# Loading the first four chunks of a gated recurrence in 112-row transfers, the first gate tensor in two column halves

## Chip, cores and metric

The kernel runs on one core of a Trainium2 chip. The metric is the device time of one execution, in microseconds. The core has five engines that work side by side: TensorE (PE; its weight loads are listed as PEld), VectorE (DVE), ScalarE (ACT), GpSimd (POOL) and SyncE (SP), which here issues all transfers between device memory and the on-chip memory. Sixteen DMA engines carry the transfers. On-chip tiles have up to 128 partitions (rows).

## What is computed

A gated linear recurrence for 4 batches and 8 heads, 768 steps of 48 channels, and then a multiplicative feed-forward block (FFN) on 3072 tokens of width 384:

```python
f = 1.0 / (1.0 + np.exp(-f_logit))
state = zeros((B, H, D, D))
for t in range(S):
    state = f[:, :, t, :, None] * state + np.einsum('bhd,bhe->bhde', k[:, :, t], v[:, :, t])
    y[:, :, t] = np.einsum('bhd,bhde->bhe', q[:, :, t], state)
x = y.transpose(0, 2, 1, 3).reshape(B * S, H * D)
a = x @ w1
b = x @ w2
out = ((a * b) @ w3) @ w_out
```

The kernel cuts each sequence into chunks of 128 steps, 24 chunks in all (6 for each batch). In a chunk it multiplies q by the running product of the gates from the chunk's start (a forward scan), and k by the running product toward the chunk's end (a backward scan), so that the products within a chunk become matmuls under a causal mask, and only one state passes from chunk to chunk. w3 and w_out are folded into one matrix on the chip.

## The kernel before

The inputs q, k and f_logit lie in device memory as `[chunk, 2, 48, 512]`: the heads in two groups (even and odd, `par`), 48 channels each, and for every channel 4 heads x 128 steps. On the chip a chunk's tile has R = 112 rows: group 0 in rows 0 to 47, group 1 in rows 64 to 111. Rows 48 to 63 belong to neither group; their results are not used, but what stands in them goes through the scans and products, so they are filled with values that do no harm (0 for q and k, 30 for f). The first four chunks have tiles of their own, so that all their loads can be issued at the start.

A small planner (`plan.add(engine, cost, emit, deps, prio)`) lays all work out in time by the estimated costs and emits it engine by engine in that order; the costs in the code are its estimates. The two functions that matter here are `setup`, with the fills, and `front`, with the loads, the sigmoid, the scans and the two products. The loads of one core's SyncE are tied to eight completion semaphores in turn: the ninth load waits until the first has landed.

```python
def rows(par):
    return slice(64 * par, 64 * par + D)
# ...
    floor = keep.tile([R, NQ], F32, name="floor")
    back = keep.tile([R, NQ], F32, name="back")
    gate = [keep.tile([R, NQ + 1], F32, name=f"gate{i}") for i in range(2)]
    qs, ks, fs = ([keep.tile([R, NQ], F32, name=f"{nm}{i}") for i in range(n)] for nm, n in (("q", 3), ("k", 2), ("f", 2)))
    # ...
    def idle(n):

        to = ps_f.tile([P, TB], F32, name=f"f{NF - 1}")[:, 0:TH]
        for _ in range(n):
            nc.tensor.matmul(to, lhsT=floor[:, 0:P], rhs=floor[:, 0:TH], start=True, stop=True)

    plan.add("PE", 7.8, lambda: idle(9), prio=-1e8)

    def setup():
        nc.scalar.activation(warm, nc.const_aps.tensor(0.0, (R, 1), F32), AF.Sigmoid)
        for i in range(2):
            if i == 0:
                nc.gpsimd.memset(ks[i][32:64], 0.0)
                nc.gpsimd.memset(qs[i][32:64], 0.0)
                make_identity(nc, ident)
            else:
                nc.gpsimd.memset(fs[i][32:64], 30.0)
        nc.gpsimd.memset(early[32:64, 2:4], 30.0)
        nc.gpsimd.memset(early[32:64, 0:2], 0.0)
        nc.gpsimd.memset(qs[2][32:64], 0.0)
        nc.gpsimd.memset(qs[3][32:64], 0.0)
        nc.vector.memset(floor, FLOOR)
        nc.vector.memset(heads(floor)[:, :, 0], 1.0)
        nc.vector.memset(back, 0.0)
        for t in gate:
            nc.vector.memset(t[:, NQ : NQ + 1], 0.0)
        nc.vector.memset(ks[1][32:64], 0.0)
        nc.vector.memset(qs[1][32:64], 0.0)
        for t in sb:
            nc.vector.memset(t, 0.0)

        nc.gpsimd.memset(perm, 0.0)
        # ... ten copies of parts of ident into perm, on GpSimd
    def moves(n, size, rate, emit, deps, prio, late=0.0):


        for j in range(n):
            i = plan.add("SP", 0.45, (lambda: None) if j else emit, [d] if j else deps, prio - j * 1e-3, takes=["lane"], lag=0.6)
            d = i
            t = plan.add("DMA", size / n / rate, lambda: None, [i], prio - j * 1e-3, lag=1.3 + late, frees=[i])
        return t

    def front(u):

        s, t = st[u], tk[u]
        n0 = need(u)

        def load(dst, src):
            def emit():
                if dst is fs[0] and u == 0:

                    nc.sync.dma_start(dst[0:64], src[u].rearrange("two d n -> (two d) n")[0:64])
                    nc.sync.dma_start(dst[rows(1)], src[u, 1])
                    return
                for par in range(2):
                    nc.sync.dma_start(dst[rows(par)], src[u, par])
            return emit

        fu, qu, ku = (x[u if u < 4 else u % n] for x, n in ((fs, 2), (qs, 3), (ks, 2)))

        def free(n, *names):

            if u < 4:
                return []
            return asked[8:9] + [tk[u - n if u - n >= 4 else u % n][nm] for nm in names]

        t["lf"] = moves(2, 197, 250, load(fu, f_logit), free(2, "g"), n0 - 30)
        t["lk"] = moves(2, 197, 250, load(ku, k), free(2, "k"), n0 - 29.5)
        t["lq"] = moves(2, 197, 250, load(qu, q), free(3, "q"), n0 - 29)

        def load_v():
            s["v"] = at(12288 + NQ, DM) if u == 3 else loads.tile([P, DM], F32, name="vt")
            loaded(s["v"], u)

        t["lv"] = moves(
            1 if u < NPE else 3, 197, 320, load_v, [] if u == 3 else past(u, 4 if u in (4, 5, 6) else 3, "v", "s"),
            n0 - (28.2, 28.2, 28.2, 29.6, 12)[min(u, NPE)],
        )

        def gates():
            nc.scalar.activation(gate[u % 2][:, 0:NQ], fu, AF.Sigmoid)

        t["g"] = plan.add("ACT", 0.65, gates, [t["lf"]] + past(u, 2, "r") + past(u, 3, "G"), n0)
        if u % NCH and "G" in tk[u - 1]:
            tk[u - 1]["G"]["deps"].append(t["g"])

        def forward():
            s["P"] = one.tile([R, NQ], F32, name="fwd")
            nc.vector.tensor_tensor_scan(s["P"], gate[u % 2][:, 0:NQ], floor, 0.0, ALU.mult, ALU.max)

        t["p"] = plan.add("DVE", 1.25, forward, [t["g"]] + past(u, 1, "q", "i", "l"), n0)

        def last():
            nc.scalar.copy(lasts[:, u], heads(s["P"])[:, :, C - 1])

        t["l"] = plan.add("ACT", 0.2, last, [t["p"]], n0)

        def ends():
            nc.vector.reciprocal(heads(back)[:, :, C - 1], heads(s["P"])[:, :, C - 1])

        t["i"] = plan.add("DVE", 0.18, ends, [t["p"]] + past(u, 1, "r"), n0)

        def scale_q():
            s["Q"] = work3.tile([R, NQ], F32, name="Q")
            nc.vector.tensor_tensor(s["Q"], qu, s["P"], ALU.mult)

        t["q"] = plan.add("DVE", 0.7, scale_q, [t["p"], t["lq"]] + past(u, 3, "v", "a"), n0 + 0.1)

        def backward():
            s["R"] = one.tile([R, NQ], F32, name="bwd")
            nc.vector.tensor_tensor_scan(
                s["R"][:, ::-1], gate[u % 2][:, NQ:0:-1], back[:, ::-1], 0.0, ALU.mult, ALU.max
            )

        t["r"] = plan.add("DVE", 1.25, backward, [t["i"]] + past(u, 1, "k"), n0)

        # ... K = k * R (VectorE), then pairs(u): K^T Q on PE into pa; A = copy of pa (ScalarE);
        # causal select on A (GpSimd); values, from_state, update (PE); S, G, sb: the running state;
        # moved (PE, with perm) and settled (ScalarE): xt, the input of the FFN
# ...
    setup()
    for u in range(NU):
        if u <= NPE:
            front(u)
        if u >= NPE:
            if not (u > NPE and together(u - 1)):
                begin(u)
            if u + 1 < NU:
                front(u + 1)
        rest(u)
        if u == NPE - 1:
            weights()
        if u == NU - 1:
            looked = plan.add("DVE", 1.0, judge, [tk[i]["y"] for i in range(NU)], -20)
            sent = moves(1, 0.4, 250, told, [looked], 0, 20.0)
            judged = plan.add("DVE", 0.2, decided, [moves(1, 0.4, 250, heard, [sent], 0, 20.0)], -20)
        if u % UB == UB - 1:
            ffn(u // UB)
    ready_at = 0.0
    for t in plan.order():
        if t["eng"] == "PE" and t["at"] < FULL:
            n = int((t["at"] - ready_at) / 0.43)
            if ready_at and n:
                idle(n)
            ready_at = t["end"]
        plan.got = t.get("got")
        t["emit"]()
    return blk[NB - 1]["outside"]
```

D = 48, R = 112, C = 128, NQ = 512, HP = 4, NPE = 4, NU = 24, FLOOR = 2^-60. `idle` gives PE matmuls whose result is never read, to keep it at work before the first real ones.

Of the kernel before, what the change touches and what calls it, by code (L numbers as in the profile page):

```python
# [36 lines left out]
F32 = mybir.dt.float32  # L37
# [3 lines left out]
ALU = mybir.AluOpType  # L41
AF = mybir.ActivationFunctionType
# [3 lines left out]
P = 128  # L46
# [4 lines left out]
R = 64 + D  # L51
# [138 lines left out]
def rows(par):  # L190
    return slice(64 * par, 64 * par + D)
# [15 lines left out]
def ranged(ctx, tc, q, k, f_logit, v, w1, w2, w3, w_out, out, ident, w12, wc, left):  # L207
# [65 lines left out]
    def idle(n):  # L273

        to = ps_f.tile([P, TB], F32, name=f"f{NF - 1}")[:, 0:TH]
        for _ in range(n):
            nc.tensor.matmul(to, lhsT=floor[:, 0:P], rhs=floor[:, 0:TH], start=True, stop=True)

    plan.add("PE", 7.8, lambda: idle(9), prio=-1e8)

    def heads(t):
        return t.rearrange("p (h c) -> p h c", c=C)

    def setup():
        nc.scalar.activation(warm, nc.const_aps.tensor(0.0, (R, 1), F32), AF.Sigmoid)
        for i in range(2):
            if i == 0:
                nc.gpsimd.memset(ks[i][32:64], 0.0)
                nc.gpsimd.memset(qs[i][32:64], 0.0)
                make_identity(nc, ident)  # L290
            else:
                nc.gpsimd.memset(fs[i][32:64], 30.0)
        nc.gpsimd.memset(early[32:64, 2:4], 30.0)
        nc.gpsimd.memset(early[32:64, 0:2], 0.0)
        nc.gpsimd.memset(qs[2][32:64], 0.0)
        nc.gpsimd.memset(qs[3][32:64], 0.0)
        nc.vector.memset(floor, FLOOR)
        nc.vector.memset(heads(floor)[:, :, 0], 1.0)
        nc.vector.memset(back, 0.0)
        for t in gate:  # L300
            nc.vector.memset(t[:, NQ : NQ + 1], 0.0)
        nc.vector.memset(ks[1][32:64], 0.0)
        nc.vector.memset(qs[1][32:64], 0.0)
        for t in sb:
            nc.vector.memset(t, 0.0)

        nc.gpsimd.memset(perm, 0.0)
        for i, (kc, hp) in enumerate(met):
            for par in range(2):
                for r, t, at_, n in runs(2 * hp + par):  # L310
                    if t == kc:
                        a = 64 * par + at_
                        nc.gpsimd.tensor_copy(perm[:, i, r : r + n], ident[0:R, a : a + n])
# [22 lines left out]
# [8 lines that stand above are left out]
# [11 lines left out]
    def front(u):  # L355

        s, t = st[u], tk[u]
        n0 = need(u)

        def load(dst, src):  # L360
            def emit():
                if dst is fs[0] and u == 0:

                    nc.sync.dma_start(dst[0:64], src[u].rearrange("two d n -> (two d) n")[0:64])
                    nc.sync.dma_start(dst[rows(1)], src[u, 1])
                    return
                for par in range(2):
                    nc.sync.dma_start(dst[rows(par)], src[u, par])  # L368
# [7 lines that stand above are left out]
                return []  # L376
            return asked[8:9] + [tk[u - n if u - n >= 4 else u % n][nm] for nm in names]

        t["lf"] = moves(2, 197, 250, load(fu, f_logit), free(2, "g"), n0 - 30)
        t["lk"] = moves(2, 197, 250, load(ku, k), free(2, "k"), n0 - 29.5)  # L380
        t["lq"] = moves(2, 197, 250, load(qu, q), free(3, "q"), n0 - 29)

        def load_v():
            s["v"] = at(12288 + NQ, DM) if u == 3 else loads.tile([P, DM], F32, name="vt")
# [4 lines that stand above are left out]
            n0 - (28.2, 28.2, 28.2, 29.6, 12)[min(u, NPE)],  # L389
        )  # L390

        def gates():
            nc.scalar.activation(gate[u % 2][:, 0:NQ], fu, AF.Sigmoid)  # L393

        t["g"] = plan.add("ACT", 0.65, gates, [t["lf"]] + past(u, 2, "r") + past(u, 3, "G"), n0)
        if u % NCH and "G" in tk[u - 1]:
            tk[u - 1]["G"]["deps"].append(t["g"])

        def forward():
            s["P"] = one.tile([R, NQ], F32, name="fwd")  # L400
            nc.vector.tensor_tensor_scan(s["P"], gate[u % 2][:, 0:NQ], floor, 0.0, ALU.mult, ALU.max)  # L401

        t["p"] = plan.add("DVE", 1.25, forward, [t["g"]] + past(u, 1, "q", "i", "l"), n0)

        def last():
            nc.scalar.copy(lasts[:, u], heads(s["P"])[:, :, C - 1])  # L406
# [22 lines that stand above are left out]
        def scale_k():  # L429
            s["K"] = work.tile([R, NQ], F32, name="K")  # L430
            if u < NPE:
                nc.vector.tensor_tensor(s["K"], ku, s["R"], ALU.mult)
                return

            kk, k_, r_ = (
                x.rearrange("p (b two h c) -> p b two h c", two=2, h=2, c=C // 2) for x in (s["K"], ku, s["R"])
            )
            nc.vector.tensor_tensor(kk[:, :, 0], k_[:, :, 0], r_[:, :, 0], ALU.mult)
            nc.vector.tensor_tensor(kk[:, :, 1, ::-1], k_[:, :, 1], r_[:, :, 1], ALU.mult)

        t["k"] = plan.add("DVE", 0.7 if u < NPE else 0.8, scale_k, [t["r"], t["lk"]] + past(u, 2, "a", "t"), n0)
        if u in (2, 3):
            t["k"]["frees"].append(coming)
# [1193 lines left out]
```

## Time and profile before

| | us |
|---|---|
| device time, median of 3 (lowest to highest) | 488.78 (488.72 to 489.14) |
| span of the profiled execution | 486.6 |
| PE busy | 475.6 (98%) |
| PEld busy | 406.9 (84%) |
| VectorE busy | 360.9 (74%) |
| ScalarE busy | 166.5 (34%) |
| GpSimd busy | 85.6 (18%) |
| DMA, share of 16 engines over the span | 34.1% |

The profile is one execution, recorded by the hardware. Times in it count from the first instruction of the span. Line numbers such as L393 are lines of this kernel. An instruction line gives engine, line, operation, the tile written, the tile read, and their shapes; a bracket at its end says how long its engine had been idle before it and what it had waited for. Some views merge neighbours of the same kind (x16). "SPq" is SyncE's queue while it issues a transfer. Shares of busy time are averages over stages that have different limits, so the stages are looked at one by one. Matmul ends are modelled, and a busy PE is not PE at its peak.

### The profile page before, as it was taken

Reading aid. Unit: us, or ns where it says so; the run is one execution under the profiler, and the core shown is the slowest. Engines: PE = TensorE matmul, PEld = TensorE weight load, DVE = VectorE, ACT = ScalarE, POOL = GpSimd, SP = SyncE. Lnnn points to the kernel's source line nnn. Section 1 sums busy time; section 2 is a strip of 40 time slices with the busy share of each in tenths; the row PEclk is TensorE's granted clock in tenths of the full one; section 3 lists DMA queues with packets and bytes.
Section 4 is the critical chain, followed back from the end, with each engine's and each line's share of the span. In section 5 each row is a group of like instructions: output and inputs, shape, how many; then the busy total and the mean of one; then the engine's idle time right before and its main releaser. Section 6 shows DMA issues by size and latency. Waiting matters only on the chain.

```text
span 486.6 us, 9566 instructions
## 1 busy us (share of the span) xinstructions
PE 475.6 (98%) x3690; PEld 406.9 (84%) x3690; DVE 360.9 (74%) x703; ACT 166.5 (34%) x380; POOL 85.6 (18%) x132
## 2 busy tenths in 40 slices
PE   7799999999999999999999999999999999999995
PEld 6698645666799888899988889988899888889995
DVE  7999989999999879989777557456663667664541
ACT  4788446663334453553533511001100110110000
POOL 9300000315233342334332200000000000000000
PEclk9999999999999999999999999999999999999998
DMA  6899476553336765465412102000011000000011
GB/s 182 288 325 263 141 274 235 190 178 83 98 83 183 193 157 137 99 165 164 119 48 48 35 17 66 32 34 1 14 52 50 16 1 0 1 1 0 34 66 39
DMA packets 44935, 50.03 MB, mean 103 GB/s; under 512 B 15426, under 2 KB 34370, under 8 KB 43858
## 3 DMA queue, kind: packets, MB, share of 16 engines
q1 hardware_dynamic: 44882, 49.34, 34.1%
q8 instruction: 31, 0.51, 0.4%
q14 instruction: 22, 0.18, 0.1%
HBM read 40.67 MB, written 8.65 MB: 101 GB/s over the span
## 4 chain that ended last, share of the span: by engine, by line
PE 88%; DVE 7%; issue 2%; DMA 1%; SPq 1%; ACT 0%; DVEq 0%; ACTq 0%
PE f L728 70%; PE f L1190 5%; PE py L498 4%; PE pa L464 2%; PE py L517 2%; PE py L476 2%; DVE place L1222 1%; PE f L531 1%; DVE fwd L401 1%; DVE bwd L423 1%; PE f L706 1%; DVE Q L417 1%; SPq L368 1%; DMA f<-in_f_logit_dram 1%; DVE place L1137 0%
## 5 line engine op out<-in xcount | busy, mean ns | idle before, releaser
L728 PE MATMUL f<-xt,w 128*128 128x256 f32 (+1 forms) x600 | 159.0, 396 | 0.0
L728 PEld LDWEIGHTS f<-xt,w 128*128 128x128 f32 x600 | 113.5, 190 | 24.8 <-issue 10.3
L728 PE MATMUL f<-place 128*128 128x192 f32 (+1 forms) x504 | 112.6, 350 | 0.2 <-DVE place L964 0.2
L728 PEld LDWEIGHTS f<-place 128*128 128x128 f32 x504 | 87.6, 190 | 6.2 <-DVE place L964 0.5
L557 POOL TENSOR_SCALAR_AFFINE_SELECT A<-A 64x256 f32<-64x256 f32 (+1 forms) x84 | 59.3, 726 | 90.7 <-ACT A L551 50.2
L1190 PE MATMUL f<-place 128*128 128x384 f32 x128 | 42.5, 489 | 0.0
L831 ACT COPY a<-f 128x256 f32<-128x256 f32 x36 | 13.4, 372 | 85.0 <-PE f L728 66.0
L1190 PEld LDWEIGHTS f<-place 128*128 128x128 f32 x128 | 23.9, 190 | 16.6 <-DVE place L1143 0.5
L728 PE MATMUL f<-xt,place 128*128 128x256 f32 x144 | 37.3, 382 | 0.0
L728 PE MATMUL f<-wc,ab 128*128 128x192 f32 x192 | 35.1, 326 | 0.0
L645 POOL TENSOR_TENSOR G<-lasts,gate 112x4 f32<-112x4 f32 x20 | 14.3, 714 | 102.7 <-ACT lasts L406 39.8
L728 PEld LDWEIGHTS f<-wc,ab 128*128 128x128 f32 x192 | 32.0, 190 | 0.4
L423 DVE TENSOR_TENSOR_SCAN bwd<-gate,back 112x512 f32<-112x512 f32 x24 | 30.2, 1256 | 0.7
L401 DVE TENSOR_TENSOR_SCAN fwd<-gate,floor 112x512 f32<-112x512 f32 x24 | 29.8, 1240 | 1.2 <-ACT gate L393 0.5
L728 PEld LDWEIGHTS f<-xt,place 128*128 128x128 f32 x144 | 26.6, 189 | 4.0 <-DVE place L855 0.5
L551 ACT COPY A<-pa 64x256 f32<-64x256 f32 (+1 forms) x60 | 24.2, 438 | 12.2 <-PE pa L464 11.4
L855 DVE TENSOR_TENSOR place<-f,a 128x256 f32<-128x256 f32 x36 | 15.2, 422 | 17.2 <-PE f L728 16.9
L667 ACT COPY sb<-S 48x192 f32<-48x192 f32 x40 | 14.0, 350 | 31.5 <-DVE S L658 24.5
L498 PEld LDWEIGHTS py<-A,vt 128*64 128x64 f32 (+1 forms) x320 | 17.5, 129 | 6.6 <-issue 6.1
L498 PE MATMUL py<-A,vt 128*64 128x128 f32 (+1 forms) x320 | 22.6, 280 | 0.0
L1126 ACT ACTIVATE place<-place 128x512 f32<-128x512 f32 (+2 forms) x24 | 21.2, 884 | 2.5 <-DVE w L1143 1.3
L728 PE MATMUL f<-place,w 128*128 128x256 f32 x72 | 21.4, 379 | 0.0
(121 smaller groups left out, 650.2 us busy)
## 6 DMA issues: line engine op xcount, KB each, us to landing
place<-in_w_dram SPq DMA_DIRECT2D x8, 1024.0 KB, 4.9
place<-in_w_dram SPq DMA_DIRECT2D x12, 512.0 KB, 10.1
out_dram<-o SPq DMA_DIRECT2D x24, 192.0 KB, 1.9
q<-in_q_dram SPq DMA_DIRECT2D x46, 96.0 KB, 2.5
k<-in_k_dram SPq DMA_DIRECT2D x44, 96.0 KB, 2.4
f<-in_f_logit_dram SPq DMA_DIRECT2D x43, 96.0 KB, 2.6
yt<-ys SPq DMA_DIRECT2D x40, 96.0 KB, 2.1
xt<-yt SPq DMA_DIRECT2D x20, 192.0 KB, 2.8
```

Source lines behind the costliest of these rows:

```text
L401: nc.vector.tensor_tensor_scan(s["P"], gate[u % 2][:, 0:NQ], floor, 0.0, ALU.mult, ALU.max)
L423: nc.vector.tensor_tensor_scan(s["R"][:, ::-1], gate[u % 2][:, NQ:0:-1], back[:, ::-1], 0.0, ALU.mult, ALU.max)
L498: nc.tensor.matmul(y_block(u, b)[64 * half : 64 * half + w], lhsT=s["v"][:, h * D : h * D + w], rhs=s["A"][:, par, hp], start=zone not in ...
L551: nc.scalar.copy(parts_of(s["A"].rearrange("p r h c -> p (r h c)"))[p0:p1, :, f], parts_of(s["pa"].rearrange("p r n -> p (r n)"))[p0:p1, : ...
L557: nc.gpsimd.affine_select(out=a, in_=a, pattern=pattern, compare_op=ALU.is_ge, fill=0.0, base=0, channel_multiplier=-1,)
L645: nc.gpsimd.tensor_tensor(s["G"], lasts[:, u], heads(gate[(u + 1) % 2][:, 0:NQ])[:, :, 0], ALU.mult)
L667: nc.scalar.copy(sb[u % 2][rows(par), :, 64 * par : 64 * par + D], s["S"][rows(par)])
L728: nc.tensor.matmul(out_, lhsT=lhs[i], rhs=rhs[i], start=start and i == 0, stop=i == len(lhs) - 1, skip_group_check=True,)
L831: nc.scalar.copy(q["a"], q["X"])
L855: nc.vector.tensor_tensor(ups["u3", k], q["Y"], q["a"], ALU.add)
L1126: nc.scalar.activation(m, hi.bitcast(F32), AF.Abs)
L1190: nc.tensor.matmul(w3s["p", jc], lhsT=w3s[jc][:, kc * P : kc * P + P], rhs=wos[:, kc], start=(kc == 0), stop=(kc == KF - 1),)
```

## The change

Two things are altered in how the first four chunks start.

First, their loads of f, k and q write all 112 rows in one transfer each. The source is described as two blocks of 56 rows, the second of which begins at row 40 of the 96: rows 0 to 55 go to partitions 0 to 55, rows 40 to 95 to partitions 56 to 111. So partitions 0 to 47 and 64 to 111 hold what they held before, and partitions 48 to 63 get real rows a second time, finite numbers whose results are not used. That does away with the fills of those rows, and with one of the two transfers for each tensor.

Second, f of the first chunk comes in two transfers of 256 columns (two heads each), and sigmoid and forward scan are done for each half on its own, so that the first can begin before the second half has landed. A scan can be cut at a head's border, as the gate factor that starts a head comes from `floor`.

Along with it, q of chunk 0 is put behind f of chunk 1 in the order of loads, and the idle matmuls at the start go from 9 to 8. The diff:

```diff
--- before.py
+++ after.py
@@ -276,31 +276,19 @@
         for _ in range(n):
             nc.tensor.matmul(to, lhsT=floor[:, 0:P], rhs=floor[:, 0:TH], start=True, stop=True)
 
-    plan.add("PE", 7.8, lambda: idle(9), prio=-1e8)
+    plan.add("PE", 6.9, lambda: idle(8), prio=-1e8)
 
     def heads(t):
         return t.rearrange("p (h c) -> p h c", c=C)
 
     def setup():
         nc.scalar.activation(warm, nc.const_aps.tensor(0.0, (R, 1), F32), AF.Sigmoid)
-        for i in range(2):
-            if i == 0:
-                nc.gpsimd.memset(ks[i][32:64], 0.0)
-                nc.gpsimd.memset(qs[i][32:64], 0.0)
-                make_identity(nc, ident)
-            else:
-                nc.gpsimd.memset(fs[i][32:64], 30.0)
-        nc.gpsimd.memset(early[32:64, 2:4], 30.0)
-        nc.gpsimd.memset(early[32:64, 0:2], 0.0)
-        nc.gpsimd.memset(qs[2][32:64], 0.0)
-        nc.gpsimd.memset(qs[3][32:64], 0.0)
+        make_identity(nc, ident)
         nc.vector.memset(floor, FLOOR)
         nc.vector.memset(heads(floor)[:, :, 0], 1.0)
         nc.vector.memset(back, 0.0)
         for t in gate:
             nc.vector.memset(t[:, NQ : NQ + 1], 0.0)
-        nc.vector.memset(ks[1][32:64], 0.0)
-        nc.vector.memset(qs[1][32:64], 0.0)
         for t in sb:
             nc.vector.memset(t, 0.0)
 
@@ -357,12 +345,13 @@
         s, t = st[u], tk[u]
         n0 = need(u)
 
-        def load(dst, src):
+        def load(dst, src, a=0, n=NQ):
             def emit():
-                if dst is fs[0] and u == 0:
-
-                    nc.sync.dma_start(dst[0:64], src[u].rearrange("two d n -> (two d) n")[0:64])
-                    nc.sync.dma_start(dst[rows(1)], src[u, 1])
+                if u < 4:
+
+                    of = src[u, 0]
+                    of = bass.AP(tensor=of.tensor, offset=of.offset + a, ap=[[(D - 8) * NQ, 2], [NQ, D + 8], [1, n]])
+                    nc.sync.dma_start(dst[:, a : a + n], of)
                     return
                 for par in range(2):
                     nc.sync.dma_start(dst[rows(par)], src[u, par])
@@ -376,9 +365,16 @@
                 return []
             return asked[8:9] + [tk[u - n if u - n >= 4 else u % n][nm] for nm in names]
 
-        t["lf"] = moves(2, 197, 250, load(fu, f_logit), free(2, "g"), n0 - 30)
-        t["lk"] = moves(2, 197, 250, load(ku, k), free(2, "k"), n0 - 29.5)
-        t["lq"] = moves(2, 197, 250, load(qu, q), free(3, "q"), n0 - 29)
+        def load_rows(dst, src, deps, prio):
+            return moves(1, 230, 250, load(dst, src), deps, prio) if u < 4 else moves(2, 197, 250, load(dst, src), deps, prio)
+
+        if u == 0:
+            t["lf0"] = moves(1, 115, 250, load(fu, f_logit, 0, NQ // 2), [], n0 - 30.5)
+            t["lf"] = moves(1, 115, 250, load(fu, f_logit, NQ // 2, NQ // 2), [], n0 - 30)
+        else:
+            t["lf"] = load_rows(fu, f_logit, free(2, "g"), n0 - 30)
+        t["lk"] = load_rows(ku, k, free(2, "k"), n0 - 29.5)
+        t["lq"] = load_rows(qu, q, free(3, "q"), n0 - (29 if u else 28.9))
 
         def load_v():
             s["v"] = at(12288 + NQ, DM) if u == 3 else loads.tile([P, DM], F32, name="vt")
@@ -389,18 +385,27 @@
             n0 - (28.2, 28.2, 28.2, 29.6, 12)[min(u, NPE)],
         )
 
-        def gates():
-            nc.scalar.activation(gate[u % 2][:, 0:NQ], fu, AF.Sigmoid)
-
-        t["g"] = plan.add("ACT", 0.65, gates, [t["lf"]] + past(u, 2, "r") + past(u, 3, "G"), n0)
+        def gates(a=0, n=NQ):
+            nc.scalar.activation(gate[u % 2][:, a : a + n], fu[:, a : a + n], AF.Sigmoid)
+
+        def forward(a=0, n=NQ):
+            if a == 0:
+                s["P"] = one.tile([R, NQ], F32, name="fwd")
+            cols = slice(a, a + n)
+            nc.vector.tensor_tensor_scan(s["P"][:, cols], gate[u % 2][:, cols], floor[:, cols], 0.0, ALU.mult, ALU.max)
+
+        if u == 0:
+
+            g0 = plan.add("ACT", 0.38, lambda: gates(0, NQ // 2), [t["lf0"]], n0 - 1)
+            p0 = plan.add("DVE", 0.65, lambda: forward(0, NQ // 2), [g0], n0 - 1)
+        part = (NQ // 2, NQ // 2) if u == 0 else ()
+        t["g"] = plan.add("ACT", 0.38 if part else 0.65, lambda: gates(*part), [t["lf"]] + past(u, 2, "r") + past(u, 3, "G"), n0)
         if u % NCH and "G" in tk[u - 1]:
             tk[u - 1]["G"]["deps"].append(t["g"])
 
-        def forward():
-            s["P"] = one.tile([R, NQ], F32, name="fwd")
-            nc.vector.tensor_tensor_scan(s["P"], gate[u % 2][:, 0:NQ], floor, 0.0, ALU.mult, ALU.max)
-
-        t["p"] = plan.add("DVE", 1.25, forward, [t["g"]] + past(u, 1, "q", "i", "l"), n0)
+        t["p"] = plan.add(
+            "DVE", 0.65 if part else 1.25, lambda: forward(*part), [t["g"]] + ([p0] if part else []) + past(u, 1, "q", "i", "l"), n0,
+        )
 
         def last():
             nc.scalar.copy(lasts[:, u], heads(s["P"])[:, :, C - 1])
```

In the built programs the order of instructions on PE is the same before and after, but for the idle matmuls. On VectorE two fills go and the first scan becomes two instructions; on GpSimd seven fills go. On ScalarE the copy of chunk 0's masked products comes ahead of the sigmoid of chunk 2, and some of the first weight conversions move by a few places. The loads of the first four chunks go from 24 transfers for q, k and f to 13; those of v stay.

## The prediction

> **What bounds the kernel now.** I read the windows view first, then the chain that ended last, then the timeline of the first 36 us. The windows view gives for each stretch the busy time of PE, PEld, DVE, ACT and POOL with instruction counts, then the granted PE clock, the DMA share and GB/s:
>
> ```profile
> 5.00:10.00 5.00, 4.17 (x32) 3.32 (x30) 4.74 (x6) 1.36 (x3) 4.88 (x9) 1.00 0.77 216
> 10.00:15.00 5.00, 3.95 (x46) 3.12 (x44) 4.61 (x7) 3.49 (x7) 3.66 (x8) 1.00 0.81 243
> 20.00:25.00 5.00, 4.00 (x63) 3.48 (x62) 4.86 (x7) 4.53 (x10) 1.15 (x1) 1.00 1.00 383
> 30.00:35.00 5.00, 5.00 (x59) 4.65 (x55) 4.83 (x11) 4.97 (x10) 0.00 (x0) 1.00 0.88 251
> 35.00:45.00 10.00, 10.00 (x48) 8.78 (x48) 9.18 (x20) 9.23 (x19) 0.00 (x0) 1.00 0.97 261
> ```
>
> From 25 us on PE is busy for all of every stretch, but for 0.2 us near 133 us and the tail after 481 us. So the end moves one for one with the moment at which PE gets going, and only the first 25 us, which is all that the change touches, are open. There the chain is this (start, length, what):
>
> ```profile
> 1.46 2.66 DMA f<-in_f_logit_dram
> ...
> 4.21 0.64 ACT gate L393
> ...
> 4.87 1.24 DVE fwd L401
> ...
> 23.66 0.69 DVE Q L417
> ...
> 24.48 1.16 PE pa L452 x16
> ...
> 35.00 41.32 PE f L728 x144
> ```
>
> The second part of the first f lands at 4.12 us; sigmoid and scan follow at once. From 4.87 to 24.35 us VectorE is hardly idle (4.6 to 4.9 of every 5 us). The last of its work on the first four chunks is Q of chunk 3, at 23.66; with it PE begins a stretch without gaps, and at 35.00 the first FFN matmuls. Two lines of the timeline show a loss inside the DVE stretch, and two show when the queue of loads is through:
>
> ```profile
> 11.97 1.09 POOL L557 TENSOR_SCALAR_AFFINE_SELECT A<-A 128x1024 f32<-128x1024 f32 x1
> ...
> 12.33 1.27 DVE L432 TENSOR_TENSOR K<-k,bwd 112x512 f32<-112x512 f32 x1
> ...
> 13.31 0.84 SPq L368 DMA_DIRECT2D place<-in_q_dram x2
> ...
> 14.20 9.34 SPq L1107 DMA_DIRECT2D place<-in_w_dram x10
> ```
>
> K of chunk 1 takes 1.27 us where chunk 0's took 0.69, because it runs into the select. And q of chunk 3 is issued at 13.31 and landed (3.6 us later by the issue table) at some 17.3 us, over 6 us before Q needs it at 23.66. Loads are not what is waited for here, beyond the first.
>
> **What the Trainium skill says.** (1) "DMA: Bandwidth & Descriptors", section "Why a DMA increments its semaphore by 16 and not by 1": a load issued from SyncE is split over k of the 16 engines, where k is the largest number up to 16 that divides the size of the slowest dimension (not of size 1) of both access patterns; on the hardware path it is the lowest-numbered k engines. Every load of an input in the kernel before has 48, 64 or 128 rows outermost on both sides (v of later chunks 256 and 128 or 128 and 64), so k = 16 for all, and the trace agrees as far as it goes: the DMA share reaches 1.00 of 16 engines with the weights. No run here shows a load with a small outermost dimension. (2) The same page, "Specifications": about 27 GiB/s for one engine. The trace: 406 GB/s at share 1.02 from 24 to 28 us with 4 KB rows, so 25 GB/s for each engine; with the 2 KB rows of q, k and f, 229 GB/s at share 0.80 from 8 to 11 us, so 17.9 GB/s, or 114 ns for a row. (3) "SBUF — State Buffer", "Who interferes with whom": a VectorE instruction with two SBUF inputs is blocked by a GpSimd instruction that reads SBUF. The trace agrees: the K of 1.27 us above ends at 13.60, 0.54 us after the select.
>
> **The change, part by part.**
>
> *Padding fills.* Seven GpSimd fills go (5 of 0.52 and 2 of 0.94 us: 4.5 us) and two on VectorE (0.48 each). None is on the chain: VectorE was done with its setup at 4.40 and waited for the sigmoid until 4.84. A small gain further on: GpSimd's copies into the permutation ended at 11.86, and the first gains G after them held S up by 0.22 us.
>
> *First f by columns.* Alone, with loads as fast as before: the two halves land at about 3.5 and 4.1 us (2.65 us from their issues at 0.82 and 1.46). A sigmoid of 256 columns takes 0.37 (as ACT's copies of 256 columns do), a scan of 256 some 0.63 (half of 1.22 and a little): first half 3.6 to 4.0 and 4.0 to 4.65, second half 4.2 to 4.6 and 4.65 to 5.3. The scan ends at 5.3 instead of 6.1, 0.8 us earlier. Because the sequence on ScalarE also moves the copy of the first A ahead of chunk 2's sigmoid, the select comes earlier against K of chunk 1, worth another 0.3. All of it would reach 24.48 and the end: about 1.1 us, or 487.7 us in all.
>
> *All 112 rows at once.* 24 loads become 13, which spares SyncE issues of 0.42 us, and brings 17% more bytes. But look at the source pattern: `[[(D-8)*NQ, 2], [NQ, D+8], [1, n]]`. It is 2 blocks of 56 rows; the target has 112 rows. The largest number up to 16 that divides 2 and 112 is 2. By the skill's rule each of these 13 loads runs on two engines, 56 rows on each, and on the same two every time. Before, a load of 48 rows put 3 on each of 16.
>
> What a row costs on one engine with a full queue: not over 114 ns (that number counts gaps of short loads), not under 81 (2048 bytes at 25.4 GB/s). I take 90. A load of 112 x 2 KB: 56 x 0.090 = 5.0 us. Half of the first f, rows of 1 KB, I estimate at 55 ns: 3.1 us. The v loads of 128 rows have k = 16, 8 rows on each engine, 0.55 us on the two that matter, four times: 2.2 us. Fixed part of the first load: it landed 2.8 us after its issue at 0.82 with 4 rows on each engine, 4 x 0.114 = 0.46, so about 2.3. In ring order q of chunk 3 is the last of the 17:
>
> 0.82 + 2.3 + 2 x 3.1 + 11 x 5.04 + 2.2 = 67.0 us
>
> instead of some 17. All that was hidden is now exposed: VectorE's 23.66 becomes about 67, a shift of 43.3 us. What follows it is the same sequence as before (Q, pairs, copy of A, select, values, three permutations), and the weights lie in the ring behind q: their rows on the two engines come at 8 x 0.16 = 1.3 us a piece, faster than VectorE decodes them (2.12 us from one piece to the next, 30.13 to 32.25), so the 11.3 us from Q to the FFN's start should stay nearly the same. PE and VectorE then stay in step as before, with nothing in reserve to catch up: PE has no gaps to give back. The earlier sigmoid and the fills are of no more weight, as chunk 0's k lands only near 14 us. Sum: 488.8 + 43.3 = 532 us.
>
> **Rivals.** *A: all 16 engines are used after all.* The rule as I apply it needs the instruction to carry the 2 x 56 as it is written; something between the program and the engine might split the rows otherwise. Then the sum is the 1.1 us above. DMA would be the tighter resource: 3.5 MB for four chunks at 280 GB/s (216 at share 0.77) take 12.7 us, q of chunk 3 landing near 15, still before its use. Time 487.7, 486.8 to 488.8. For it: the change is plainly meant so, and the diff reckons these loads at 250 GB/s. Against it: the skill names just this case, an outermost dimension of fewer than 16.
> *B: two engines, at 114 ns a row.* Then a load is 6.4 us, with the halves and v in proportion q lands near 83 us, and the time is 549. For it: that is what the 2 KB rows took by the share. Against it: the share counts the ramps of loads with three rows to an engine.
> *C: two engines, at 75 to 81 ns a row*, if long queues bring an engine to its full rate: q lands at 56 to 61 us, and the time is 522 to 526. For it: 4 KB rows reach 25.4 GB/s in the trace. Against it: a row of 2 KB has half as many bytes to spread its own cost over.
> *D: two engines, but hidden.* It would need slack of 40 us before Q; the trace has 6. I give it nothing.
>
> **Range and chances.** B and C span 522 to 549; cold matmuls after PE's long waits, or a delay of the weights that share the two engines, add a few us, a faster row takes a few off. Range 516 to 552, point 532. That the two-engine rule applies: 0.8. Then the change is slower by 5 to 13%, far over 2%. Otherwise it is A, within 2%. Faster by over 2% would need 9.8 us out of 25 that are mostly VectorE's own work: 0.02.
>
> **What would show it.** Right: a DMA share near 2/16 = 0.13 and 40 to 50 GB/s for most of the first 65 us; loads of f, k and q each landing some 5 us after the one before, with times from issue to landing far above 2.6 us; VectorE idle in front of K and Q and ScalarE in front of its sigmoids, for DMA; the first FFN matmul near 78 us; after it the same length to the end as before. Wrong: landings of 2.5 to 4 us and a first scan that ends near 5.3 us (then A), or an FFN start that moves by much less than Q of chunk 3 does (then the step that carries the delay one for one fails).

## Result and profile after

The changed kernel takes 533.22 us (median of 4 runs, 532.82 to 533.59) against 488.96 of the kernel before: a ratio of 1.0905, 95% interval 1.0886 to 1.0924. It is slower by 44.3 us. The spans of the two profiles, 531.1 and 486.6 us, differ by 44.5.

The windows view of the kernel after, with the same columns as before (busy time and count of PE, PEld, DVE, ACT, POOL, then granted PE clock, DMA share, GB/s):

```profile
5.00:10.00 5.00, 2.75 (x10) 1.93 (x8) 1.25 (x2) 0.83 (x2) 0.00 (x0) 0.99 0.13 46
20.00:25.00 5.00, 1.08 (x10) 1.08 (x12) 1.72 (x2) 0.00 (x0) 0.00 (x0) 0.50 0.15 53
60.00:65.00 5.00, 1.18 (x22) 0.92 (x20) 0.74 (x2) 0.69 (x2) 0.79 (x1) 0.95 1.03 322
65.00:70.00 5.00, 4.90 (x37) 4.38 (x38) 3.68 (x8) 3.50 (x6) 1.09 (x1) 0.50 1.03 407
80.00:90.00 10.00, 10.00 (x48) 8.81 (x47) 8.67 (x19) 9.57 (x19) 0.00 (x0) 1.00 1.03 295
```

VectorE, busy 4.74 of 5 us from 5 to 10 us before, is busy 1.25; the DMA share is 0.13, two of sixteen. At 60 us the share is at 1 (the weights), and PE still has little to do. From 65 to 70 us it works, but at half its clock. From 75 us on it is busy again, but for short waits.

The DMA view of the first 70 us, in 40 slices, shows what the transfers move:

```profile
GB/s 0 18 36 43 48 48 49 49 49 49 50 143 48 49 49 48 49 49 50 135 71 50 50 49 54 141 49 52 147 49 49 247 231 293 313 287 359 412 393 414
```

49 GB/s is 24.5 for each of two engines. The four peaks near 140 are the v loads, whose 128 rows the prediction reckons on all sixteen; the weights follow from 54 us.

The timeline (start, length, what; in brackets the idle time of the engine before it and who ended it):

```profile
6.45 0.42 ACT L389 ACTIVATE gate<-f 112x256 f32<-112x256 f32 x1 [4.13 <-DMA f<-in_f_logit_dram]
8.99 0.42 ACT L389 ACTIVATE gate<-f 112x256 f32<-112x256 f32 x1 [2.13 <-DMA f<-in_f_logit_dram]
9.46 4.55 SPq L354 DMA_DIRECT2D k<-in_k_dram x1
13.75 0.69 DVE L437 TENSOR_TENSOR K<-k,bwd 112x512 f32<-112x512 f32 x1 [2.15 <-DMA k<-in_k_dram]
14.05 4.53 SPq L336 DMA_DIRECT2D vt<-in_v_dram x1
18.36 0.63 ACT L389 ACTIVATE gate<-f 112x512 f32<-112x512 f32 x1 [8.00 <-DMA f<-in_f_logit_dram]
23.17 0.69 DVE L422 TENSOR_TENSOR Q<-q,fwd 112x512 f32<-112x512 f32 x1 [8.73 <-DMA q<-in_q_dram]
...
64.26 0.69 DVE L422 TENSOR_TENSOR Q<-place,fwd 112x512 f32<-112x512 f32 x1 [5.89 <-DMA place<-in_q_dram]
65.10 2.08 PE L457 MATMUL pa<-Q,K 48*128 48x128 f32 x16 [3.92 <-DVE Q L422]
```

The two halves of f are in at 6.45 and 8.99, k of chunk 0 at 13.75, f of chunk 1 at 18.36, q of chunk 0 at 23.17: one load each 4.6 to 4.8 us. SyncE's issue of a load itself lasts 4.5 us, and so does that of v behind it. Q of chunk 3, the last of VectorE's work on these chunks, waits 5.89 us and starts at 64.26 instead of 23.66.

The chain that ended last goes from there to the FFN:

```profile
48.41 15.82 DMA place<-in_q_dram
...
65.10 2.08 PE pa L457 x16
67.18 1.90 PE f L503 x15
69.07 1.98 PE f L515 x8
...
78.54 38.76 PE f L733 x138
```

The pairs took 1.16 us before, here 2.08; the values (L503) and the part from the state (L515), 1.09 and 1.13 before, take 1.97 and 2.05 in the timeline (the chain counts each from the end of the piece ahead of it). The first FFN matmul starts at 78.38 instead of 34.84, by the timelines of after and before:

```profile
78.38 5.99 PE L733 MATMUL f<-xt,w 128*128 128x256 f32 x27
34.84 41.48 PE L728 MATMUL f<-xt,w 128*128 128x256 f32 x144
```

So the 44.5 us are: 40.6 until Q of chunk 3, 2.9 from there to the FFN (14.1 us instead of 11.2), and 1.0 after it.

### The profile page after: what moved, and what is told of

It reads as the page before. It is cut to its first block, busy times and chain, and to the rows that moved or that the text cites. A ratio compares the mean times of both kernels' runs of the same rounds, so it can differ in the third digit from the quotient of the medians.

```text
span 531.1 us, 9528 instructions
## 1 busy us (share of the span) xinstructions
PE 485.1 (91%) x3688; PEld 414.6 (78%) x3688; DVE 359.0 (68%) x702; ACT 166.5 (31%) x381; POOL 78.3 (15%) x125
## 4 chain that ended last, share of the span: by engine, by line
PE 80%; SPq 9%; DVE 6%; DMA 3%; issue 1%; ACT 0%; DVEq 0%
PE f L733 63%; SPq L354 5%; PE f L1195 4%; PE py L503 4%; SPq L336 3%; DMA place<-in_q_dram 3%; PE pa L469 2%; PE py L522 2%; PE py L481 2%; DVE place L1227 1%; PE f L536 1%; PE f L711 1%; DVE bwd L428 1%; DVE place L1142 1%; PE f L515 1%
## 5 line engine op out<-in xcount | busy, mean ns | idle before, releaser
L395 DVE TENSOR_TENSOR_SCAN fwd<-gate,floor 112x512 f32<-112x512 f32 (+1 forms) x25 | 29.9, 1197 | 16.1 <-ACT gate L389 10.3
L422 DVE TENSOR_TENSOR Q<-q,fwd 112x512 f32<-112x512 f32 x23 | 17.4, 755 | 13.7 <-DMA q<-in_q_dram 13.7
L503 PEld LDWEIGHTS py<-A,vt 128*64 128x64 f32 (+1 forms) x320 | 17.5, 129 | 6.6 <-issue 6.1
L503 PE MATMUL py<-A,vt 128*64 128x128 f32 (+1 forms) x320 | 22.6, 281 | 0.0
```

What stands on the lines that cost most here:

```text
L395: nc.vector.tensor_tensor_scan(s["P"][:, cols], gate[u % 2][:, cols], floor[:, cols], 0.0, ALU.mult, ALU.max)
L503: nc.tensor.matmul(y_block(u, b)[64 * half : 64 * half + w], lhsT=s["v"][:, h * D : h * D + w], rhs=s["A"][:, par, hp], start=zone not in ...
```

## Experiments

A profile is one execution, and three of them lie away from the median of their kernel: 492.51 us in the run with 64 and 48 rows (median 490.07), 490.90 with 16 x 7 (489.42), 491.53 with 8 x 14 (493.16).

**Is it the shape of the source pattern?** The theory: the outermost size of the source (2) sets how many DMA engines a load uses, and all of the loss is the row time on two engines, carried by Q of chunk 3 to the end. The rivals: the padding that is no longer filled, the halves by columns, or PE's slow clock. The first run keeps everything of the change but the shape: 64 rows of the first 96, then the 48 of the second block.

```diff
-  nc.sync.dma_start(dst[:, a:a+n], of)                      # 2 x 56 rows
+  of = src[u].rearrange("two d n -> (two d) n")
+  nc.sync.dma_start(dst[0:64, a:a+n], of[0:64, a:a+n])
+  nc.sync.dma_start(dst[rows(1), a:a+n], src[u, 1, :, a:a+n])
```

> Every load of the first four chunks as 64 rows and 48 rows (two transfers, outermost dimensions 64 and 48), all else as in the changed kernel, halves of the first f and missing fills included. My theory (two engines because the source's outermost dimension is 2): the loads are as fast as before, the four transfers of the first f eat up what the halves could gain, 488.3 us (487.5 to 489.2). Rival 'columns, order or idle matmuls': stays near 533.

Measured: 490.07 us, ratio to before 1.0023 (1.0015 to 1.0031). The 43 us are gone with the shape alone; fills and halves are as in the change. What is left over before is 1.0 us. In the execution that was profiled, SyncE issues such a pair in 0.47 + 0.58 us (two times 48 rows: 0.84), f of chunk 3 comes late, and PE has a gap:

```profile
18.96 0.63 ACT L389 ACTIVATE gate<-ab 112x512 f32<-112x512 f32 x1 [4.05 <-DMA ab<-in_f_logit_dram]
20.21 2.29 PE L711 MATMUL f<-ys,ab 112*128 112x128 f32 x12 [3.17 <-ACT ys L682]
```

There the FFN starts at 37.84, 3.0 us later than before. That this also holds for the median is not shown: some 0.9 of its 1.0 us have another source, which the last experiment below shows.

The next three keep one transfer for each load and vary the outermost size. Such blocks of equal size cannot hold the two 48-row parts as they must lie, so here the rows are overlapped differently and wrong rows stand in some partitions: these kernels do not compute the recurrence and only time the loads. Bytes, number of rows and instructions are those of the change.

```diff
-  ap=[[(D - 8) * NQ, 2], [NQ, D + 8], [1, n]]     # 2 blocks of 56 rows
+  ap=[[6 * NQ, 16], [NQ, 7], [1, n]]              # e2: 16 of 7
+  ap=[[23 * NQ, 4], [NQ, 28], [1, n]]             # e3: 4 of 28
+  ap=[[11 * NQ, 8], [NQ, 14], [1, n]]             # e4: 8 of 14
```

> One transfer of 112 rows with overlapping blocks as in the changed kernel, but 16 blocks of 7 rows that begin 6 rows apart, so the outermost dimension is 16 and the bytes are the same (the rows land in the wrong places, so the output isn't the reference's). My theory: all 16 engines, a load lands 2.6 to 3.5 us after its issue, 487.7 us (486.8 to 488.8). Rival 'the overlapping three-dimensional pattern is slow to issue (4.5 us for one issue in the trace), or the bytes and rows read twice': stays near 533.

> The same with 4 blocks of 28 rows that begin 23 rows apart (output again not the reference's). My theory: 4 engines, 98 GB/s while loads alone run, 28 rows x 81 ns = 2.3 us for a load, q of chunk 3 lands at 3.9 + 2.5 + 11 x 2.28 + 2.6 = 34 us, 10.4 us after VectorE could use it: 499 to 502 us. Rival 'slow form of issue': near 533. Rival 'anything but the row pattern': near 533.

> The same with 8 blocks of 14 rows that begin 11 rows apart (output again not the reference's). My theory: 8 engines, about 196 GB/s, 1.14 us for a load, q of chunk 3 lands near 20 us and is hidden again behind VectorE: 488.2 us (487.3 to 489.5). Rivals as before: near 533.

Measured:

| blocks x rows | GB/s while these loads run alone | Q of chunk 3 at | first FFN matmul | time, us | ratio (95%) |
|---|---|---|---|---|---|
| 2 x 56 (the change) | 49 | 64.26 | 78.38 | 533.22 | 1.0905 (1.0886 to 1.0924) |
| 4 x 28 | 98 | 37.96 | 51.22 | 506.11 | 1.0342 (1.0323 to 1.0361) |
| 8 x 14 | about 200 | 24.88 | 36.87 | 493.16 | 1.0081 (1.0060 to 1.0102) |
| 16 x 7 | not alone long enough | 23.22 | 35.98 | 489.42 | 1.0005 (0.9997 to 1.0013) |
| before (48, 64 rows) | | 23.66 | 34.84 | 488.8 to 489.1 | 1 |

The bandwidth doubles with the number of blocks, 24.5 GB/s to each. In the DMA view of 4 x 28, first 30 us in 40 slices:

```profile
GB/s 0 0 0 20 94 72 93 91 85 105 187 194 96 98 98 98 98 98 98 115 279 98 98 98 98 98 98 160 234 119 121 252 106 98 115 202 333 220 272 317
```

and of 8 x 14, first 40 us:

```profile
GB/s 0 0 50 129 124 201 197 204 220 194 261 172 240 225 283 157 209 329 263 259 285 256 277 311 410 397 414 414 410 401 426 378 257 357 315 252 211 196 97 255
```

This is the count that the Trainium skill gives ("DMA: Bandwidth & Descriptors", "Why a DMA increments its semaphore by 16 and not by 1"): the largest number up to 16 that divides the outermost sizes of both sides. The runs agree at 2, 4 and 8. The two middle times were missed upwards. With 4 x 28 q of chunk 3 was expected at 34 us and Q starts at 37.96; most of that lies in the last two loads and two v, beside the weights: 8.50 us from f of chunk 3 (29.46) to Q, where 5.9 were reckoned. And Q moved by 14.3 us but the FFN by 16.4: PE was at half its clock from 30 to 40 us after a gap of 6.26, which the expectation left out. With 8 x 14 the sigmoids wait 1.5 to 2.5 us for f: eight engines were taken to be hidden and are not quite.

**Is PE's slow clock the rest of the way from Q to the FFN?** The change, with 14 idle matmuls (two for each of seven, as in the kernel's own start) ahead of the pairs of chunk 3:

```diff
+  if t is tk[3]["a"]:
+      idle(7)
   t["emit"]()
```

> The changed kernel with 14 idle matmuls put on PE ahead of the pairs of chunk 3, where it had been idle for 3.9 us and then ran the next 5 us at half its clock. If the 2.9 us by which the way from Q of chunk 3 to the FFN grew (14.1 us after, 11.2 before) are the slow clock: 530.4 us (529.6 to 531.5). If they are the weights that land late behind q in the same two engines (ScalarE waited 4.0 us for them): unchanged, 533.

Measured: 531.27 us, ratio 1.0858 (1.0842 to 1.0874), 2.0 below the change. The window in which the change had a clock of 0.50:

```profile
65.00:70.00 5.00, 5.00 (x51) 4.22 (x50) 3.31 (x8) 3.53 (x6) 0.85 (x1) 1.00 1.00 374
```

Though its idle matmuls ended only at 66.80 and Q of chunk 3 came 0.4 later than in the change, the FFN starts at 77.16, 1.2 earlier:

```profile
66.80 1.16 PE L457 MATMUL pa<-Q,K 48*128 48x128 f32 x16
...
77.16 7.07 PE L733 MATMUL f<-xt,w 128*128 128x256 f32 x32
```

From the pairs to the FFN it is 10.36 us here, 10.36 before (24.48 to 34.84) and 13.28 in the change (65.10 to 78.38). So the slow clock is the whole of the 2.9 us, and the idle matmuls win back less because the pairs have to wait for their end. The same was tried with 16 x 7 (six idle matmuls ahead of the pairs), to see whether the clock had eaten the earlier scan's gain:

> The 16 x 7 form (all 16 engines, output not the reference's) with 6 idle matmuls ahead of the pairs of chunk 3, where PE stood still for 1.6 us and then ran at half clock. If that gap ate what the earlier first scan gained: 487.6 us (486.8 to 488.3), below the kernel before. If the gain was lost in VectorE's waits or locks: 489.2, as without them.

Measured: 489.62 us, ratio 1.0009 (1.0002 to 1.0015). The clock in the profile stayed at 1.00 and nothing was gained in the median. Over the whole span the profiled execution of 16 x 7 had a mean clock of 0.994, its 13 others 0.996 to 0.999, so the half clock in that profile can hardly be in its median, and there was little to save. This theory fell for that kernel.

**Does the place of a load decide what two engines cost?** Before, with one single load in the 2 x 56 form: q of chunk 3, which before has over 6 us in reserve, or f of chunk 0, which has none.

```diff
+  if u == 3 and src is q:          # e8; in e9: if dst is fs[0] and u == 0
+      of = bass.AP(..., ap=[[(D - 8) * NQ, 2], [NQ, D + 8], [1, NQ]])
+      nc.sync.dma_start(dst[0:R], of)
+      return
```

> The kernel before with one load alone in the 2 x 56 form, q of chunk 3. My theory: two engines, 4.6 us for it, landed by about 20 us, still ahead of its use at 23.7 us: hidden, 489.1 us (488.4 to 490.2). Rival 'such a load slows every load after it as well': 493 or more.

> The kernel before with one load alone in the 2 x 56 form, f of chunk 0, which the first sigmoid waits for. My theory: it lands at about 8.3 us instead of 4.1 and the 4.2 us reach the end in full: 493.3 us (492.3 to 495).

Measured: q of chunk 3: 489.67 us, ratio 1.0011 (1.0005 to 1.0018); Q of chunk 3 starts at 23.48, without a wait. But the load is not quite hidden: the weights lie behind it in the queue, and in the profile their conversion on ScalarE starts at 24.41, after a wait, instead of 21.87. PE then waits for the select, and the FFN starts at 35.93, 1.1 us later than before:

```profile
24.41 0.68 ACT L1131 ACTIVATE place<-place 128x512 f32<-128x512 f32 x1 [2.62 <-DMA place<-in_w_dram]
30.48 1.09 PE L503 MATMUL f<-A,place 128*64 128x128 f32 x16 [1.21 <-POOL A L562]
```

f of chunk 0: 495.9 us, 1.0139 (1.0123 to 1.0154), more than expected. In the timeline of the second:

```profile
9.72 1.23 DVE L402 TENSOR_TENSOR_SCAN fwd<-gate,floor 112x512 f32<-112x512 f32 x1 [5.32 <-ACT gate L394]
...
13.34 0.98 PE L477 MATMUL py<-ident,K 112*128 112x112 f32 x4 [4.45 <-DVE K L433]
```

The scan is 4.85 us late. After 4.45 us without work PE ran at half clock (0.50 from 15 to 20 us), VectorE then waited for its products, and the pairs of chunk 3 start at 31.89 instead of 24.48, 7.4 late. So the same load costs under 1 us or 7 us by its place, and a late first load costs half as much again as its own delay.

**What are the halves by columns worth, undone alone in the change?**

```diff
-  t["lf0"] = moves(1, 115, 250, load(fu, f_logit, 0, NQ // 2), [], n0 - 30.5)
-  t["lf"] = moves(1, 115, 250, load(fu, f_logit, NQ // 2, NQ // 2), [], n0 - 30)
+  t["lf"] = t["lf0"] = moves(1, 230, 250, load(fu, f_logit), [], n0 - 30)    # one sigmoid, one scan
```

> The changed kernel with the first f in one load of 2 x 56 rows and one sigmoid and scan, so without the halves by columns. If the two-engine shape is the whole of the loss, and the loads in ring order set Q of chunk 3, the halves are of no weight: the load of f takes 4.6 us as a whole instead of 2 x 2.5, so q of chunk 3 lands up to 0.4 us earlier, and the time is 532.5 to 533.5. If the halves mattered either way, it would differ by over 1 us.

Measured: 530.52 us, ratio 1.0862 (1.0847 to 1.0878): 2.7 us better than the change, where under 1 was expected. On two engines the halves are a loss. In the timeline and the windows of this run:

```profile
8.13 0.63 ACT L388 ACTIVATE gate<-f 112x512 f32<-112x512 f32 x1 [5.82 <-DMA f<-in_f_logit_dram]
...
63.86 1.96 PE L456 MATMUL pa<-Q,K 48*128 48x128 f32 x16 [3.00 <-DVE Q L421]
```

```profile
66.00:68.00 2.00, 2.00 (x20) 1.74 (x18) 1.90 (x4) 1.91 (x4) 0.00 (x0) 0.64 0.95 338
68.00:70.00 2.00, 2.00 (x21) 2.00 (x20) 0.52 (x2) 1.53 (x5) 1.15 (x1) 1.00 0.91 316
```

The whole f is in at 8.13, the second half at 8.99; of that 0.86 becomes 1.24 at Q of chunk 3 (63.02). In the two profiles the other 1.3 us are clock again (11.96 us from the pairs to the FFN, in the change 13.28): PE is back at full speed before 68 us, some 4 us after its start, in the change only near 71, some 6 us after. That the halves bring the later return about is not shown.

**Is there a gain in the earlier scan at all?** In the 16 x 7 run the first scan ended at 5.26 us instead of 6.10, as the prediction had worked out for fast loads, and the time did not move. Three runs look for where that goes. First, before with only the 48 lower rows of the first f on ScalarE's queue, so that f lands sooner:

```diff
+  nc.scalar.dma_start(fs[0][rows(1)], f_logit[0, 1])   # first of ScalarE's work
-  nc.sync.dma_start(dst[rows(1)], src[u, 1])
```

> The kernel before, with the 48 lower rows of the first f issued on ScalarE's queue beside SyncE's 64 rows instead of 0.64 us after them. If the landing of the first f alone opens the busy stretch of VectorE, f is in at some 3.5 us, the first scan starts at 4.40, where VectorE's setup ends, instead of 4.87, and the time is 488.3 to 488.7 against 488.9 or so. If the gain is lost on the way to Q of chunk 3, as in the run with blocks of 7 rows, the time stays within 0.2 us. If ScalarE's table load of 1.28 us comes before its issue, f lands later than before and the time rises by up to 0.6.

Measured: 488.56 us, before 488.85, ratio 0.9992 (0.9984 to 1.0001). In the timeline:

```profile
3.74 0.63 ACT L393 ACTIVATE gate<-f 112x512 f32<-112x512 f32 x1 [1.00 <-DMA f<-in_f_logit_dram]
4.40 1.22 DVE L401 TENSOR_TENSOR_SCAN fwd<-gate,floor 112x512 f32<-112x512 f32 x1
...
23.18 0.68 DVE L417 TENSOR_TENSOR Q<-place,fwd 112x512 f32<-112x512 f32 x1
```

4.40 against 4.87, 23.18 against 23.66, the FFN at 34.36 against 34.84: one for one all the way, 0.3 in the medians. (Single profiles differ here by themselves: in the run with q of chunk 3 in 2 x 56, whose first f is loaded as before, the first scan starts at 4.56.) It is the only version with a median below the kernel before, and the interval just reaches 1. Second, the same with halves by columns, on sixteen engines (k and q of chunk 1 in 64 + 48 rows, to spare VectorE two fills):

```diff
+  nc.scalar.dma_start(fs[0][rows(1), 0:256], f_logit[0, 1, :, 0:256])     # and 256:512
+  nc.sync.dma_start(dst[0:64, a:a+n], src[u].rearrange(...)[0:64, a:a+n]) # a = 0, 256
```

> The kernel before with the first f by columns in two halves and a sigmoid and a scan for each, as in the change, but in rows of 64 (SyncE's queue) and 48 (ScalarE's), so on 16 engines; k and q of chunk 1 take 64 of 96 rows and 48, which spares VectorE two fills. It is the good part of the change without its shape. Estimate: first half in at 3.4, first scans 3.8 to 5.2 us where before has 4.87 to 6.10: 0.9 us, so 488.0 if it all arrives. If the first 25 us give it back to waits further on, 488.5 to 489.5.

Measured: 490.25 us, ratio 1.0028 (1.0017 to 1.0039). The first scans end at 5.29, 0.8 us earlier, but the sequence that results leaves less for the loads further on:

```profile
13.55 1.80 PE L468 MATMUL pa<-Q,K 48*128 48x128 f32 x16 [1.55 <-DVE Q L433]
14.47 0.63 ACT L400 ACTIVATE gate<-ab 112x512 f32<-112x512 f32 x1 [2.88 <-DMA ab<-in_f_logit_dram]
```

The sigmoid of chunk 3 waits for f (before had it at 13.71), PE falls to a clock of 0.77 between 15 and 20 us, and the FFN starts at 35.44. Third, 16 x 7 with q of chunk 0 again ahead of f of chunk 1, because Q of chunk 0 had waited 0.52 us for it:

```diff
-  t["lq"] = load_rows(qu, q, free(3, "q"), n0 - (29 if u else 28.9))
+  t["lq"] = load_rows(qu, q, free(3, "q"), n0 - 29)
```

> The run with blocks of 7 rows on 16 engines, with q of chunk 0 issued ahead of f of chunk 1 as in the kernel before (its output is not the reference's). There Q of chunk 0 had waited 0.52 us for its load. If that order ate the gain of the earlier scan, Q of chunk 3 comes at 22.7 and the time at 488.2 to 488.8; if the gain goes to waits further on, it stays at 489.0 to 489.6.

Measured: 488.9 us, ratio 0.9999 (0.9991 to 1.0007). Here Q of chunk 3 starts at 22.81 and the FFN at 33.99, 0.85 earlier than before. The span, 486.5 us, is the same, since PE now waits in the middle of the next stage, where it had not before:

```profile
75.82 5.40 PE L1195 MATMUL f<-place 128*128 128x384 f32 x16 [0.34 <-ACT place L1134]
81.42 2.85 PE L1195 MATMUL f<-place 128*128 128x384 f32 x8 [0.21 <-DVE place L1148]
```

It looks as if the decoding of weights on ScalarE and VectorE stood close behind as the next limit. The other traces say otherwise. The change has the same two waits, though its FFN starts 44 us later:

```profile
120.20 5.40 PE L1195 MATMUL f<-place 128*128 128x384 f32 x16 [0.34 <-ACT place L1134]
125.81 5.43 PE L1195 MATMUL f<-place 128*128 128x384 f32 x16 [0.21 <-DVE place L1148]
```

And the way from the first FFN matmul to the next place at which PE waits in all kernels does not depend on when the FFN starts, but on the kernel (before, 16 x 7 with q of chunk 0 first, the change):

```profile
133.54 1.57 PE L728 MATMUL f<-place 128*128 128x192 f32 x8 [0.20 <-DVE place L964]
133.56 1.57 PE L733 MATMUL f<-place 128*128 128x192 f32 x8 [0.19 <-DVE place L969]
177.96 1.57 PE L733 MATMUL f<-place 128*128 128x192 f32 x8 [0.21 <-DVE place L969]
```

| kernel | first FFN matmul | this matmul | between, us |
|---|---|---|---|
| before | 34.84 | 133.54 | 98.70 |
| before, lower rows of the first f on ScalarE's queue | 34.36 | 133.06 | 98.70 |
| before, f of chunk 0 in 2 x 56 | 42.24 | 140.94 | 98.70 |
| 16 x 7, q of chunk 0 first | 33.99 | 133.56 | 99.57 |
| 16 x 7 | 35.98 | 135.56 | 99.58 |
| the change | 78.38 | 177.96 | 99.58 |
| halves on two queues | 35.44 | 135.41 | 99.97 |

All nine traces of kernels made from the change with its order of work lie at 99.56 to 99.58, the four with that of before at 98.70 to 98.71; the run with halves on two queues, with an order of its own, takes 1.27 us more than before. So some 0.87 us are not the price of an earlier start: they come with the order in which the planner lays the changed kernel's work on ScalarE and VectorE. For one, before converts a piece of w_out on ScalarE at 59.33, ahead of a copy that waits for PE until 63.48; in the changed kernels this conversion stands behind the copy. PE's two waits are 0.55 of the 0.87; the rest shows no wait, and no run changed this order alone. The earlier scan thus does bring 0.85 us to the FFN's start, and the changed order takes them back. What the good part of the change is worth with the order of before was not run.

## Why the prediction was right, point by point

*What bounds the kernel.* Right. The run with the lower rows on ScalarE's queue moves the first scan by 0.47, Q of chunk 3 by 0.48 and the FFN by 0.48; the load of f alone in 2 x 56 moves them the other way. One statement was too generous: that loads beyond the first are not waited for holds for before, but f of chunk 3 has almost no reserve; it ended the wait of a sigmoid as soon as the work got 0.5 us earlier (at 13.65, in the run with two queues) or its issue later.

*Two engines.* Right, and shown rather than argued: 49, 98 and 200 GB/s at 2, 4 and 8 blocks, and with the shape taken back 1.0 of the 44 us is left. Rival A (sixteen engines after all) and D (hidden) are out. Even for q of chunk 3 alone D is right only as far as Q: the weights behind it come later, and 0.6 us are lost.

*The sum for q of chunk 3.* 67.0 us predicted, 64.26 measured (the start of Q, which follows the landing at once). Its terms:

| term | predicted | measured |
|---|---|---|
| issue at 0.82 to second half of f | 8.5 (2.3 + 2 x 3.1) | 8.17 (8.99 - 0.82) |
| one half of f after the other | 3.1 | 2.54 (45 ns a row) |
| eleven loads and four v | 57.6 (11 x 5.04 + 2.2) | 55.3 (64.26 - 8.99) |

The eleven loads were too dear: between f of chunk 1 (18.36) and f of chunk 3 (52.19) lie seven loads and two v; with 0.6 us for a v (estimated from the 5.2 us for v and q of chunk 2 against 4.6 without v) a load is 4.66 us, 83 ns a row instead of 90. The fixed part went the other way: the first half was in 5.6 us after its issue, not 5.4. The last two loads, beside the weights, took 1.5 us more than that pace. Rival B's 114 ns is out: it counted the ramps of short loads. C's 75 to 81 was close to the row; what its 56 to 61 us lacked most of all is that time beside the weights.

*From Q of chunk 3 to the FFN.* This step failed: "the 11.3 us from Q to the FFN's start should stay nearly the same". It became 14.1 (11.2 before in the same view). PE had nothing to do for 3.92 us before the pairs and ran at half clock for some 6 us. Pairs, values and state part took 0.92, 0.88 and 0.92 us more than before, together 2.7. The text named cold matmuls as a risk for the range, but not as a term; it should have been one, since a PE that waits for each load was part of the same prediction. The two errors, -2.7 in the loads and +2.9 in the clock, cancel. That 532.0 lies 1.2 us from 533.2 is partly luck.

*After the FFN's start.* Nearly right: 452.7 us instead of 451.8. Of this 1.0 us, 0.88 is the other order on ScalarE and VectorE (99.58 us instead of 98.70 in the table above). "PE has no gaps to give back" overlooked that the change could bring new ones.

*Fills and halves.* That the fills lie beside the chain is in agreement with the 16 x 7 run with q of chunk 0 first, which has none: its FFN gains 0.85 us, and its first scan alone, which the halves bring forward, 0.86. Of the 1.1 us that the prediction gave the change with fast loads, the first 0.8 appear at the first scan as worked out (5.26), and at the FFN 0.85 in the best order of loads; in the time nothing of it. "All of it would reach 24.48 and the end" failed on the order of work: the gain reached the FFN, and the changed order took back 0.87 after it. That the halves were of no weight beside the slow loads was wrong by 2.7 us: they made the first f 0.9 us later, and in the profile PE's clock came back later.

What stays open: which instruction's new place costs the 0.87 us, and whether the change without it, on sixteen engines, would run below the kernel before.

## What to carry to other kernels

Before merging two loads into one, look at the outermost size of the pattern on both sides: with 2 blocks of 56 rows the load ran at 49 GB/s, with 4 at 98, with 8 at 200, and a row-by-row pattern was worth more than half the number of issues. Price a slow load by where it stands: the same form cost under 1 us late in the queue and 7 us as the first load. When a stage becomes a wait for loads, add to its sum the matmuls that follow at half clock, and when a head start does not reach the end, compare the later stages in the traces of all kernels, the slower ones too: here a wait that looked like the next limit turned out to belong to the changed order of work.

## What the runs showed of the hardware that was not expected

- SyncE's issue of a load, 0.6 us when the queue is free, lasted 4.5 us when two engines had the earlier loads still to move (k of chunk 1 at 9.46: 4.55 us), and the issue of v, which has 128 rows outermost, was held up as long behind it (14.05: 4.53 us).
- How long PE stays at half clock after a gap varies: some 4 us after a gap of 3.00 us, some 6 after one of 3.92. The Trainium skill ("TensorE: Matmul & The Clock Gate", "Part 1: The HAM clock gate (the "warmup" mystery)") speaks of windows of about 3.4 us that run freely, so that the moment depends on where in the window the work begins; the two values lie between one such window and two. But half clock came after a gap of 1.62 us in the profile of the 16 x 7 run and after one of 1.55 us in that of the halves on two queues, while gaps of 1.00 us in the kernel before and in four of the runs brought none. Each profile is a single execution, and no threshold follows from them.
- A row of 1 KB took 45 ns on an engine with a full queue (22.8 GB/s), one of 2 KB 83 ns (24.7 GB/s): nearly in proportion to the bytes.
